# Set attention and a gated MLP on one core: three jobs of GpSimd given to VectorE, one sum in a bank of its own, the maxima of batches 1 to 3 without TensorE

## The chip, the core and the metric

The kernel runs on one core of a Trainium2 chip. A time is the device time of one execution in microseconds (us), the median of several. PE is TensorE, DVE VectorE, ACT ScalarE, POOL GpSimd, and SP the engine whose queue issues all DMAs here.

## The reference, cut to what matters

```python
B, N, m, C = 4, 12480, 32, 128          # x: (B, N, C); inducing: (m, C), float32

def mab(q, kv):
    s = (q @ kv.T) / sqrt(C)
    a = exp(s - s.max(-1));  a /= a.sum(-1) + 1e-9
    return a @ kv

h   = mab(inducing, x)                   # first attention: 32 queries over 12480 rows, for each batch
t   = mab(x, h)                          # second attention: 12480 queries over 32 rows
u   = t @ w_in                           # (49920, 128) @ (128, 2048)
out = (u * sigmoid(1.702 * u)) @ w_out   # (49920, 2048) @ (2048, 128)
```

`w_in` and `w_out` are float64, and the kernel takes each as a pair of 32-bit words and makes float32 of it on the chip ("decoding"). The product with `w_in` is folded into the second attention: `h @ w_in` is 32 rows a batch, so a token block's `u` is its 32 weights times that.

## The kernel before

**Tiling.** A batch's 12480 tokens are six "sups" of 2048 tokens and one of 192. The main work is 96 blocks of 512 tokens and 2 joint blocks of leftovers, each in 8 steps of two 128-column chunks of the 2048. In a step PE makes `ph` from the stacked weights `st` and `hw` (L484), ACT takes the gelu `g` (L508), ACT (L524) or DVE (L531) rounds it to `hi`, DVE takes the rest `lo` (L540), and PE adds three products per chunk into `pso` (L598 to L600). The first 12 steps use one full float32 product instead (L584).

**Order.** Nothing is scheduled on the chip. A planner in the kernel (`Plan`) holds jobs, each with an engine, an estimated time (`occ`, `lat`), a rank, a `wait` and a `gate`, and writes each engine's instructions out in the order in which its own clock would start them. `URGE` is how much earlier a job counts than it is ready, `BESIDE` lengthens a DVE job while POOL is at work, `counts["F"]` is the number of steps whose L484 is out. DVE, ACT and SP work in that order, one instruction after another.

**Opening** (batch 0). Transposed rows of `x` come by DMA; PE makes scores (`scores_of`, L302), DVE their maxima (L1213), PE and DVE spread the maximum of each of four `GROUPS` of sups (`group`, L1280 to L1292), ACT takes exponentials (L1304), DVE transposes them (L1317), and PE weighs the rows (`weigh`, L321) into `heap`, one PSUM bank in which each group has 128 columns. The rows in natural order (`xf`) are turned by PE and copied by ACT (`turn_of_x`, L1237, L1244), but for sup 5, which comes by a DMA (L1036). `combine` then adds the four sums with a factor each (L1353, L1355) and divides them (L1366). Beside this runs `weights(k)` for 8 pieces of 512 columns: seven operations of DVE, two of ACT and two of POOL (L1155, L1156; L1158 for the last).

**Batches 1 to 3** (`attention(b)`), spread among the steps: scores and maxima, then the maximum over sups and four partition groups, by DVE (L721), a PE product with the identity (L727), four operations of DVE on one row (L733, L737), a PE product back (L743) and one scaling (L749); then exponentials (L761), transposes (L781) and the weighing (L321), for which `loads_x` requests rows `xn` by DMA (L639), two sups at a time, in a ring of two buffers.

**Second attention** (`second`, `lay_out`): PE scores (L310); DVE transpose and maximum (L888, L895); POOL subtracts (L901); ACT exponentials (L926); DVE sums and inverts (L955 to L957); POOL scales, rounds and takes the rest (L967 to L969); DVE transposes both halves (L974, L977) into a ring `two` of two buffers; SP stacks them by 16 DMAs (L995). This is done for 27 parts, 23 of them of 512 columns and 4 small.

Of the kernel before, what the change touches and what calls it, by code (L numbers as in the profile page):

```python
# [10 lines left out]
F32R = mybir.dt.float32r  # L11
AF = mybir.ActivationFunctionType
# [4 lines left out]
P = 128  # L17
# [17 lines left out]
ROWS = 5,  # L35


def LOADS(xs, ws, n):
    return [xs[1], xs[2], ws[0], xs[3], ws[1], xs[4], xs[6], xs[5], *n, *ws[2:]]
# [4 lines left out]
URGE = 200.0  # L44
# [5 lines left out]
class Unit:  # L50


    def __init__(self, uses=1, ap=None, ready=None, parts=1):
        self.ap, self.uses, self.ready = ap, uses, ready
        self.parts = 0 if ready is not None else parts
        self.done, self.gone = 0.0, None
        self.by, self.soon = None, 0.0

# [50 lines left out]
class Plan:  # L109
# [4 lines left out]
    BESIDE = 0.34  # L114
# [39 lines left out]
    def step(self):  # L154
# [35 lines left out]
        if job.eng == "DVE":  # L190
            more = self.BESIDE * max(0.0, min(job.occ, self.free["POOL"] - s))
# [10 lines left out]
        for u in (*job.writes, *job.joins, *(u for _, u in job.takes)):  # L202
            u.made(job.eng, s + job.occ + more, end)
# [26 lines left out]


def on_pool(n):
    return 150 + 2.6 * n, 250 + 2.6 * n
# [3 lines left out]
def set_attention_then_moe(ctx: ExitStack, tc, xT, x, indT, w_in, w_out, outT):  # L237
# [77 lines left out]
    def weigh(pa, s, aT, xn, i, n):  # L315

        t0, g, w = sups[s]
        q = 32 * g
        for kk in range(w // 32):
            j = i % G  # L320
            pe_.matmul(  # L321
                pa[32 * j:32 * j + 32, 0:P], aT[0:q, kk, :], xn[0:q, kk],
                start=(i < G), stop=(i >= n - G),
            )
            i += 1
        return i
# [70 lines left out]
    x_units[0, 1].uses = 3  # L397
# [21 lines left out]
    r_2 = Ring(2, of_pool(p2, [P, TOK], "two", "two"))  # L419
# [212 lines left out]
    def loads_x(b, units, i0):  # L632
        for s in range(NS):
            t0, g, w = sups[s]
            u = units[s]
            for j in range(g):
                def emit(u=u, t0=t0, w=w, j=j):
# [7 lines left out]
                    rank=(1, b), gate=lambda: "n" in pools and counts["F"] >= i0, size=w * 512,  # L645
# [12 lines left out]
    def attention(b):  # L658
# [16 lines left out]
        yield Job("DVE", set_clear, 100, 200, rank=filler(), wait=tarry, gate=since(i0))  # L675
        s1 = [Unit(1) for _ in range(NS)]
# [40 lines left out]
        mx1 = psm.tile([P, 1], F32, tag="mx1", name="mx1")  # L717
        m1u, rowu, pa1, pa2 = Unit(), Unit(), Unit(), Unit()

        def most():  # L720
            dve.tensor_reduce(mx1, mx, axis=AX.X, op=ALU.max)  # L721

        yield Job("DVE", most, 100, 300, done, [], rank=filler(), wait=tarry)
        m1u.at(plan.free["DVE"] + 200)

        def turn():
            pe_.matmul(pa1.ap[0:1, 0:P], mx1, ident, start=True, stop=True)  # L727

        yield Job("PE", turn, 500, 700, [m1u], [], [(r_pa, pa1)], rank=(0, 0), slack=late(600, 1500))
        row = psm.tile([1, G, M], F32, tag="row", name="row", bufs=1)  # L730

        def rows():
# [6 lines left out]
        yield Job("DVE", rows, 600, 750, [pa1], rank=filler(), wait=tarry)  # L739
        rowu.at(plan.free["DVE"] + 150)  # L740

        def back():
            pe_.matmul(pa2.ap[:, 0:1], row.rearrange("p g m -> p (g m)"), one, start=True, stop=True)  # L743

        yield Job("PE", back, 450, 650, [rowu], [], [(r_pa, pa2)], rank=(0, 0), slack=late(600, 1500))
        nmx = psm.tile([P, 1], F32, tag="nmx", name="nmx")

        def least():
            dve.tensor_scalar(nmx, pa2.ap[:, 0:1], -scale, None, op0=ALU.mult)  # L749

        yield Job("DVE", least, 100, 250, [pa2], rank=filler(), wait=tarry)
# [19 lines left out]
        xn = [Unit(parts=sups[s][1]) for s in range(NS)]  # L771
        aT = [Unit() for _ in range(NS)]
        plan.spawn(loads_x(b, xn, i0 + 40))
# [98 lines left out]
    def second(b, *parts):  # L872
# [3 lines left out]
        for some in parts:  # L876
# [3 lines left out]
            def out(s, pa, u, due=due):  # L880
# [22 lines left out]
                occ, lat = on_pool(w)  # L903
                yield Job("POOL", less, occ, lat, [m2], [e], rank=(1, 0))
# [35 lines left out]
    def lay_out():  # L940

        for key in turns[1:]:
# [20 lines left out]
            ah, ahT, alT = Unit(1), Unit(2 * g), Unit(2 * g)  # L963

            def divide():
# [5 lines left out]
            yield Job("POOL", divide, 600 + 8.5 * w, 700 + 8.5 * w, [sm], [e], [(r_tr, ah)], rank=(0, 0))  # L971

            def turn_h():
                dve.transpose(ahT.ap[0:q, 0:w], ah.ap[0:q, 0:w].bitcast(F32))  # L974

            def turn_l():
                dve.transpose(alT.ap[0:q, 0:w], e.ap[0:q, 0:w])  # L977

            yield Job("DVE", turn_h, *on_dve(w), [ah], [], [(r_2, ahT)], **by_then(due), slack=late(300, 1200))
            yield Job("DVE", turn_l, *on_dve(w), [e], [], [(r_2, alT)], **by_then(due))  # L980
            for j in range(g):
# [9 lines left out]
                for r in range(G):  # L991
                    src = alT if r % 2 else ahT

                    def emit(st=st, r=r, j=j, at=at, w=w, src=src):
                        nc.sync.dma_start(  # L995
                            st.ap[32 * r:32 * r + 32, at:at + w].bitcast(F32),
                            src.ap[32 * j:32 * j + 32, 0:w],
# [12 lines left out]
    def opening_loads():  # L1010
# [19 lines left out]
        for what, k in order:  # L1030
            if what == "n":
# [13 lines left out]
                else:  # L1045
                    plan.spawn(iter([job]))
            elif what == "x":
# [19 lines left out]
    def divided(c, cols):  # L1067
        due = 16 + 2 * c - 4
# [7 lines left out]
        def top():  # L1076
            act.copy(wh.rearrange("p c d -> p (c d)")[:, cols], wf[:, cols])

        def rest():
            dve.tensor_sub(wlf[:, cols], wf[:, cols], whf[:, cols].bitcast(F32))  # L1080

        u = Unit()
        yield Job("ACT", top, *on_act(512), [wf_units[c]], [], joins=[w_out_units[c], u], rank=rank, wait=tarry, gate=since(due))
        yield Job("DVE", rest, *on_dve(512), [u], [], joins=[w_out_units[c]], rank=rank, wait=tarry)

    def weights(k):
# [8 lines left out]
        whole = inner or c < WHOLE  # L1095
        into, done = (w_in_sb, w_in_units[c]) if inner else (wf, wf_units[c]) if whole else (whf, w_out_units[c])
# [10 lines left out]

        def square():
# [4 lines left out]
        def low_1():  # L1113
            dve.tensor_scalar(t.ap, hi(), 0x1FF, 12, op0=ALU.bitwise_and, op1=ALU.logical_shift_left)

        yield Job("DVE", low_1, 360, 470, [raw], takes=[(rings["t"], t)], rank=rank, wait=tarry)

        def low_2():
            dve.scalar_tensor_tensor(lo(), lo(), 20, t.ap, op0=ALU.logical_shift_right, op1=ALU.bitwise_or)

        yield Job("DVE", low_2, 610, 730, [], [t, raw], rank=rank, wait=tarry)

        def floats():
            act.activation(lo_f(), lo(), AF.Copy, scale=2.0 ** -32)

        low = Unit()
        plan.spawn(iter([Job("ACT", floats, 530, 700, [], [raw], joins=[low], rank=rank, wait=tarry)]))

        def top_1():
            dve.tensor_scalar(t.ap, hi(), 3, 0x3FFFF000, op0=ALU.logical_shift_left, op1=ALU.bitwise_and)  # L1130

        yield Job("DVE", top_1, 360, 450, [raw], [t], rank=rank, wait=tarry)
# [7 lines left out]
        def guard():  # L1140
            dve.scalar_tensor_tensor(
                into[:, cols], sq.ap, LEAST, t.ap.bitcast(F32), op0=ALU.is_ge, op1=ALU.mult
            )

        yield Job("DVE", guard, 610, 730, [sq, t], [], joins=[top] + [done] * (not whole), rank=rank, wait=tarry)
        sq.used(0.0)

        def powers():
            dve.tensor_scalar(hi(), into[:, cols].bitcast(I32), -(1 << 23), None, op0=ALU.bitwise_and)
# [3 lines left out]
        def lower():  # L1153
            if whole:
                nc.gpsimd.tensor_mul(hi_f(), lo_f(), hi_f())  # L1155
                nc.gpsimd.tensor_add(into[:, cols], into[:, cols], hi_f())  # L1156
            else:
                nc.gpsimd.tensor_mul(wlf[:, cols], lo_f(), hi_f())  # L1158

        cost = 3500 if whole else 1750  # L1160
        yield Job("POOL", lower, cost, cost + 150, [low, raw, raw], joins=[done], rank=rank)
        if whole and not inner:
            plan.spawn(divided(c, cols))
        decoded[0] += 1
        decoded[1] += at < SPLIT
# [32 lines left out]
    def scores_of(s):  # L1198
# [10 lines left out]
        occ = 4.1 * w * 0.42  # L1209
# [5 lines left out]
        yield Job("DVE", most, *on_dve(w), [pa], [], joins=[mx_units[s]], rank=(0, 1 + s))  # L1215
# [8 lines left out]
    def turn_of_x(s):  # L1224
# [4 lines left out]
        for k0 in range(0, w // 32, 8):  # L1229
# [10 lines left out]
            yield Job("PE", emit, 112 * n_, 112 * n_ + 250, there, [], [(r_ph, ph)], rank=(2, s), wait=350.0)  # L1240
# [23 lines left out]
    heap = Unit(99)  # L1264
# [3 lines left out]
    def group(g):  # L1268
# [4 lines left out]
        urge = -URGE if last else 0.0  # L1273
# [50 lines left out]
    def weighs():  # L1324
        for g in groups:
# [3 lines left out]
            for s in order:  # L1329
                def emit(s=s, i=i, nb=nb, g=g):  # L1330
                    a = aT_units[s].ap.rearrange("p (k m) -> p k m", m=M)
                    i[0] = weigh(heap.ap[:, g * P:(g + 1) * P], s, a, xf_units[s].ap, i[0], nb)

                occ = 67.0 * (sups[s][2] // 32)
# [320 lines left out]
```

## Time and profile before

| | us |
|---|---|
| median of 3 runs (1601.36 to 1602.05) | 1601.56 |
| the profiled execution | 1601.29 |
| its span, first to last instruction | 1599.2 |
| PE busy | 1575.1 |
| DVE busy | 1358.1 |
| ACT busy | 1319.7 |
| POOL busy | 176.5 |

The 2.1 us between the profiled execution's time and its span lie before the first and behind the last instruction. A busy PE is not PE at its peak: a matmul's record is longer than the distance to the next.

### The profile page before, as it was taken

To read this page: it belongs to the slowest core of one execution; us is meant where nothing else is said; L and a number is where in the kernel's file an instruction comes from. 1 tells how busy PE (TensorE), PEld (TensorE's weight loads), DVE (VectorE), ACT (ScalarE), POOL (GpSimd) and SP (SyncE) were. 2 spreads that over 40 slices of the span, in tenths; PEclk is the share of its full clock that TensorE was granted. 3 is DMA by queue.
4 is the path that set the end of the run, shared out by engine and by line. 5 is a ranking of instruction groups with operands and counts; after the bars stand their busy time and mean duration, and the time that the engine had idled before them with its cause. 6 is when DMAs were issued, how large, how long until landed. Compare 5 with 4: busy or idle time off the path is not lost. (4 is left out here: it accounts for less than half of the span.)

```text
span 1599.2 us, 21638 instructions
## 1 busy us (share of the span) xinstructions
PE 1575.1 (98%) x7715; PEld 1224.2 (77%) x7715; DVE 1358.1 (85%) x1537; ACT 1319.7 (83%) x1490; POOL 176.5 (11%) x129
## 2 busy tenths in 40 slices
PE   8899999999999999999999999999999999999998
PEld 6467777778887787787777777788778888888887
DVE  6989888888887888879889888788888888888886
ACT  5688888888888888788888888788988888888886
POOL 1321011020210100102011001011110110110100
PEclk9999999999999999999999999999999999999999
DMA  6262174431124226442013274410101101111100
GB/s 253 92 226 72 48 129 87 144 106 40 45 75 144 60 60 117 97 126 86 27 47 134 87 138 77 124 34 27 40 25 47 38 30 37 40 34 33 40 27 20
DMA packets 83435, 124.55 MB, mean 78 GB/s; under 512 B 12096, under 2 KB 50560, under 8 KB 77952
## 3 DMA queue, kind: packets, MB, share of 16 engines
q1 hardware_dynamic: 83328, 123.17, 27.9%
q8 instruction: 62, 1.02, 0.3%
q14 instruction: 45, 0.37, 0.1%
HBM read 69.91 MB, written 25.56 MB: 60 GB/s over the span
## 5 line engine op out<-in xcount | busy, mean ns | idle before, releaser
L540 DVE TENSOR_TENSOR lo<-g,hi 128x1024 fp32r<-128x1024 f32 (+1 forms) x772 | 965.0, 1262 | 167.2 <-ACT hi L524 153.4
L508 ACT ACTIVATE g<-ph 128x1024 f32<-128x1024 f32 (+1 forms) x784 | 801.9, 1029 | 231.3 <-PE ph L484 122.1
L598 PE MATMUL pso<-hi,wl 128*128 128x512 f32 (+1 forms) x1544 | 608.3, 394 | 0.0
L600 PE MATMUL pso<-hi,wh 128*128 128x512 f32 (+1 forms) x1544 | 606.5, 393 | 0.0
L599 PE MATMUL pso<-lo,wh 128*128 128x512 f32 (+1 forms) x1544 | 604.4, 391 | 0.8 <-DVE lo L540 0.8
L484 PE MATMUL ph<-st,hw 128*128 128x512 f32 x1536 | 473.0, 400 | 6.8 <-DVE hw L1438 2.2
L524 ACT ACTIVATE hi<-ph 128x1024 fp32r<-128x1024 f32 x458 | 469.5, 1029 | 2.8 <-PE pso L600 2.4
L484 PEld LDWEIGHTS ph<-st,hw 128*128 128x128 f32 x1536 | 280.5, 188 | 104.8 <-ACT hi L524 15.3
L598 PEld LDWEIGHTS pso<-hi,wl 128*128 128x128 f32 x1544 | 290.1, 188 | 70.1 <-issue 2.9
L600 PEld LDWEIGHTS pso<-hi,wh 128*128 128x128 f32 x1544 | 290.6, 188 | 66.1
L599 PEld LDWEIGHTS pso<-lo,wh 128*128 128x128 f32 x1544 | 290.4, 188 | 65.7 <-DVE lo L540 1.1
L531 DVE CAST hi<-g 128x1024 fp32r<-128x1024 f32 (+1 forms) x314 | 222.7, 709 | 27.7 <-ACT g L508 17.3
L967 POOL TENSOR_TENSOR e<-e,sm 128x512 f32<-128x512 f32 x23 | 36.5, 1588 | 1068.4 <-DVE sm L957 1068.4
L560 ACT COPY ob<-pso 128x512 f32<-128x512 f32 x73 | 43.4, 595 | 13.9 <-PE pso L600 13.8
L969 POOL TENSOR_TENSOR e<-e,t 128x512 f32<-128x512 f32 x23 | 45.3, 1969 | 1.8
L901 POOL TENSOR_TENSOR e<-e,m 128x512 f32<-128x512 f32 x23 | 32.3, 1406 | 58.0 <-DVE m L895 57.0
L968 POOL CAST t<-e 128x512 fp32r<-128x512 f32 x23 | 32.3, 1404 | 1.5
L563 DVE COPY ob<-pso 128x512 f32<-128x512 f32 (+1 forms) x25 | 17.1, 683 | 10.4 <-PE pso L600 9.9
L302 PE MATMUL pa<-xt,indT_sb 128*32 128x512 f32 x192 | 23.7, 599 | 0.7 <-DMA xt<-in_xT 0.7
L321 PE MATMUL pa<-xn,t 128*32 128x128 f32 (+1 forms) x594 | 19.5, 275 | 4.2 <-DMA xn<-in_x 4.2
L310 PE MATMUL pa<-xt,hT 128*32 128x512 f32 x184 | 22.9, 599 | 0.0
L584 PE MATMUL pso<-g,wf 128*128 128x512 f32 x48 | 22.7, 594 | 0.0
(170 smaller groups left out, 482.9 us busy)
## 6 DMA issues: line engine op xcount, KB each, us to landing
xt<-in_xT SPq DMA_DIRECT2D x42, 1024.0 KB, 6.5
out_T<-ob SPq DMA_DIRECT2D x96, 256.0 KB, 2.0
st<-two SPq DMA_DIRECT2D x368, 64.0 KB, 2.0
xn<-in_x SPq DMA_DIRECT2D x72, 256.0 KB, 6.4
hw<-t SPq DMA_DIRECT2D x48, 64.0 KB, 2.7
raw<-in_w_in SPq DMA_DIRECT2D x4, 512.0 KB, 9.1
raw<-in_w_out SPq DMA_DIRECT2D x4, 512.0 KB, 5.3
xt<-in_xT SPq DMA_DIRECT2D x2, 512.0 KB, 3.9
```

What stands on the lines that cost most here:

```text
L484: pe_.matmul(ph[:, c, at:at + w], u.ap[:, ch % 4 * P:(ch % 4 + 1) * P], st[:, at:at + w], start=True, stop=True,)
L508: act.activation(gs[i].ap[:, :, 0:w], phs[i].ap[:, :, 0:w], AF.Gelu_apprx_sigmoid)
L524: act.activation(his[i].ap[:, :, 0:w], phs[i].ap[:, :, 0:w], AF.Gelu_apprx_sigmoid)
L531: dve.tensor_copy(his[i].ap[:, :, 0:w], gs[i].ap[:, :, 0:w])
L540: dve.tensor_sub(los[i].ap[:, :, 0:w], gs[i].ap[:, :, 0:w], his[i].ap[:, :, 0:w].bitcast(F32))
L560: act.copy(ob.ap[:, 0:w], pso.ap[:, 0:w])
L598: pe_.matmul(o, wl[:, ch, :], hi, start=(ch == 0), stop=False)
L599: pe_.matmul(o, wh[:, ch, :], lo, start=False, stop=False)
L600: pe_.matmul(o, wh[:, ch, :], hi, start=False, stop=(ch == NCH - 1))
L901: nc.gpsimd.tensor_sub(e3, e3, m2.ap[0:q, 0:k].unsqueeze(2).broadcast_to([q, k, M]))
L967: nc.gpsimd.tensor_mul(e3, e3, sm.ap[0:q, 0:nb].unsqueeze(2).broadcast_to([q, nb, M]))
L969: nc.gpsimd.tensor_sub(e.ap[0:q, 0:w], e.ap[0:q, 0:w], ah.ap[0:q, 0:w].bitcast(F32))
```

## The change

1. `weights`: POOL's two operations go to DVE, and the two DVE operations that joined the low bits (L1114, L1119) go: ACT now reads 16 of the low word's bits (`lo_16`). The last piece is decoded into a temporary and split afterwards as the others are (`divided`).
2. `second` and `lay_out`: subtraction and scaling go to DVE; the scaled weights are transposed once, ACT (or DVE) rounds the result, DVE takes the rest in place. POOL has no work left.
3. Opening: the last group's sum goes to a buffer of its own (`tail`, of the ring that `ph` uses); half of sup 4's rows comes by a DMA of 1024 rows of 512 bytes (`HALF`) in place of 8 PE transposes and an ACT copy; the last group's maxima count as urgent.
4. `attention`: four DVE reductions of 32 partitions each, one over their results and four scalings in place of L721 to L749; `loads_x` may be placed from step `i0 + 40` on, ahead of the maxima in the thread, and the planner reckons its DMAs 2.4 times as long.
5. The planner: `URGE` 200 to 500, `BESIDE` gone, 110 ns (`AFTER`) between a DVE result and a DVE job that uses it, some PE times.

```diff
-URGE = 200.0
+URGE = 500.0
-    BESIDE = 0.34
+    AFTER = 110.0
...
+    return [xs[1], xs[2], ws[0], xs[3], ws[1], xs[4], xs[6], xs[5], *n, ("h", HALF), *ws[2:]]
...
-                    rank=(1, b), gate=lambda: "n" in pools and counts["F"] >= i0, size=w * 512,
+                    rank=(1, b), gate=lambda: "n" in pools and counts["F"] >= i0, size=2.4 * w * 512,
...
+        xn = [Unit(parts=sups[s][1]) for s in range(NS)]
+        plan.spawn(loads_x(b, xn, i0 + 40))
...
         def most():
-            dve.tensor_reduce(mx1, mx, axis=AX.X, op=ALU.max)
...
-            pe_.matmul(pa1.ap[0:1, 0:P], mx1, ident, start=True, stop=True)
...
-            dve.tensor_reduce(
-                row[:, 0, :], pa1.ap[0:1, 0:P].rearrange("p (g m) -> p m g", g=G), axis=AX.X, op=ALU.max
-            )
-            for j in range(1, G):
-                dve.tensor_copy(row[:, j, :], row[:, 0, :])
...
-            pe_.matmul(pa2.ap[:, 0:1], row.rearrange("p g m -> p (g m)"), one, start=True, stop=True)
...
-            dve.tensor_scalar(nmx, pa2.ap[:, 0:1], -scale, None, op0=ALU.mult)
+            for j in range(G):
+                dve.tensor_reduce(tops[:, j:j + 1], mx[M * j:M * j + M], axis=AX.X, op=ALU.max)
+            dve.tensor_reduce(tops[:, G:G + 1], tops[:, 0:G], axis=AX.X, op=ALU.max)
+            for j in range(G):
+                dve.tensor_scalar(nmx[M * j:M * j + M], tops[:, G:G + 1], -scale, None, op0=ALU.mult)
...
-                    nc.gpsimd.tensor_sub(e3, e3, m2.ap[0:q, 0:k].unsqueeze(2).broadcast_to([q, k, M]))
+                    dve.tensor_sub(e3, e3, m2.ap[0:q, 0:k].unsqueeze(2).broadcast_to([q, k, M]))
...
-                nc.gpsimd.tensor_mul(e3, e3, sm.ap[0:q, 0:nb].unsqueeze(2).broadcast_to([q, nb, M]))
-                nc.gpsimd.tensor_copy(ah.ap[0:q, 0:w], e.ap[0:q, 0:w])
-                nc.gpsimd.tensor_sub(e.ap[0:q, 0:w], e.ap[0:q, 0:w], ah.ap[0:q, 0:w].bitcast(F32))
...
-                dve.transpose(ahT.ap[0:q, 0:w], ah.ap[0:q, 0:w].bitcast(F32))
...
-                dve.transpose(alT.ap[0:q, 0:w], e.ap[0:q, 0:w])
...
+                dve.tensor_mul(e3, e3, sm.ap[0:q, 0:nb].unsqueeze(2).broadcast_to([q, nb, M]))
...
+                dve.transpose(aT.ap[0:q, 0:w], e.ap[0:q, 0:w])
...
+                act.copy(ah.ap[0:q, 0:w], aT.ap[0:q, 0:w])
...
+                dve.tensor_sub(aT.ap[0:q, 0:w], aT.ap[0:q, 0:w], ah.ap[0:q, 0:w].bitcast(F32))
...
+                rows = x[t0 + g * w // 2:t0 + g * w, :]
+                nc.sync.dma_start(u.second, rows.rearrange("(k p) c -> p k c", p=P))
...
-            dve.tensor_scalar(t.ap, hi(), 0x1FF, 12, op0=ALU.bitwise_and, op1=ALU.logical_shift_left)
...
-            dve.scalar_tensor_tensor(lo(), lo(), 20, t.ap, op0=ALU.logical_shift_right, op1=ALU.bitwise_or)
...
-            act.activation(lo_f(), lo(), AF.Copy, scale=2.0 ** -32)
+            act.activation(lo_f(), lo_16(), AF.Copy, scale=2.0 ** -36)
...
-                nc.gpsimd.tensor_mul(hi_f(), lo_f(), hi_f())
-                nc.gpsimd.tensor_add(into[:, cols], into[:, cols], hi_f())
+            dve.tensor_mul(lo_f(), lo_f(), hi_f())
...
+            dve.tensor_add(into(), into(), lo_f())
...
+    def sum_of(g):
+        if g == groups[-1]:
+            return tail.ap.rearrange("p c t -> p (c t)")[:, 0:P]
+        return heap.ap[:, g * P:(g + 1) * P]
```

## Rows read from the trace of the kernel before

**Rows 1.** The page: span, and each engine's busy time and instructions.
```profile
span 1599.2 us, 21638 instructions
PE 1575.1 (98%) x7715; PEld 1224.2 (77%) x7715; DVE 1358.1 (85%) x1537; ACT 1319.7 (83%) x1490; POOL 176.5 (11%) x129
```

**Rows 2.** Busy time of each engine in four stretches, granted clock, DMA share, GB/s.
```profile
0.00:37.00 37.00, 32.13 (x386) 24.39 (x387) 22.88 (x71) 21.97 (x39) 5.41 (x10) 1.00 0.74 274
37.00:80.00 43.00, 36.19 (x137) 18.66 (x136) 40.40 (x74) 28.27 (x40) 15.25 (x12) 1.00 0.24 86
80.00:100.00 20.00, 18.54 (x92) 9.71 (x92) 16.82 (x24) 18.00 (x22) 9.89 (x9) 1.00 0.72 258
100.00:1590.00 1490.00, 1483.22 (x7084) 1167.72 (x7083) 1277.96 (x1372) 1250.84 (x1390) 145.96 (x99) 1.00 0.27 71
```

**Rows 3.** PE's waits from 100 us on: total, times, longest.
```profile
PE pa L321 <- DMA xn<-in_x: 4.2, 2, 2.3
...
PE pso L599 <- DVE lo L540: 0.8, 1, 0.8
```

**Rows 4.** Timeline of PE, 210 to 232 us: start, duration, idle before.
```profile
212.78 0.39 PE L599 MATMUL pso<-lo,wh 128*128 128x512 f32 x1
213.00 0.40 PE L600 MATMUL pso<-hi,wh 128*128 128x512 f32 x1
213.33 0.38 PE L727 MATMUL pa<-ident,mx 128*1 128x128 f32 x2
213.64 1.20 PE L484 MATMUL ph<-st,hw 128*128 128x512 f32 x4
...
217.53 0.38 PE L743 MATMUL pa<-one,row 1*128 1x1 f32 x2
...
230.42 1.08 PE L321 MATMUL pa<-xn,t 128*32 128x128 f32 x32 [2.32 <-DMA xn<-in_x]
```

**Rows 5.** Timeline of SP's queue, 195 to 245 us.
```profile
216.90 6.54 SPq L639 DMA_DIRECT2D xn<-in_x  x8
```

**Rows 6.** Busy time and granted clock behind that wait.
```profile
231.50:235.50 4.00, 4.00 (x12) 3.14 (x12) 3.36 (x5) 1.94 (x2) 0.00 (x0) 0.57 1.24 189
```

**Rows 7.** Timeline of DVE, 0 to 60 us.
```profile
17.21 0.43 DVE L1130 TENSOR_SCALAR t<-raw 128x512 int32<-128x512 int32 x1
...
24.43 0.23 DVE L1281 TENSOR_SCALAR tops<-mask,mx 128x4 f32<-128x4 f32 x1
...
27.61 0.64 DVE L1213 TENSOR_REDUCE mx<-pa 128x1 f32<-128x512 f32 x1
...
28.48 0.77 DVE L1281 TENSOR_SCALAR tops<-mask,mx 128x4 f32<-128x4 f32 x1
...
33.41 0.35 DVE L1353 TENSOR_SCALAR hu<-pso,factor 128x128 f32<-128x128 f32 x1 [0.67 <-PE pso L321]
...
35.04 0.35 DVE L1355 SCALAR_TENSOR_TENSOR hu<-pso,factor,hu 128x128 f32<-128x128 f32 x1
```

**Rows 8.** Timeline of PE, 0 to 65 us.
```profile
25.79 1.06 PE L302 MATMUL pa<-xt,indT_sb 128*32 128x512 f32 x8
...
35.53 0.46 PE L1366 MATMUL pa<-rsb,hu 128*128 128x128 f32 x2 [0.88 <-DVE hu L1355]
```

**Rows 9.** Groups by line and shape, whole run: busy us, mean ns, idle before.
```profile
L540 DVE TENSOR_TENSOR lo<-g,hi 128x1024 fp32r<-128x1024 f32 x756 | 949.6, 1269 | 162.8 <-ACT hi L524 149.4 <-PE pso L600 1.1 <-issue 0.2
...
L974 DVE STREAM_TRANSPOSE two<-t 128x512 f32<-128x512 f32 x23 | 16.1, 700 | 0.0
...
L1130 DVE TENSOR_SCALAR t<-raw 128x512 int32<-128x512 int32 x8 | 7.0, 880 | 0.2
L1119 DVE SCALAR_TENSOR_TENSOR raw<-raw,t 128x512 int32<-128x512 int32 x8 | 7.0, 878 | 0.3
...
L851 DVE TENSOR_TENSOR t<-pa,t 128x512 f32<-128x512 f32 x3 | 2.0, 683 | 0.0
```

**Rows 10.** Timeline of DVE, 1300 to 1320 us, where POOL rests.
```profile
1300.02 1.23 DVE L540 TENSOR_TENSOR lo<-g,hi 128x1024 fp32r<-128x1024 f32 x1 [0.59 <-ACT hi L524]
```

More of the change, by code (lines that the diff above doesn't have):

```diff
@@ L202, in step @@
         for u in (*job.writes, *job.joins, *(u for _, u in job.takes)):
-            u.made(job.eng, s + job.occ + more, end)
+            u.made(job.eng, s + job.occ + more + self.AFTER * (job.eng == "DVE"), end)
         for u in job.reads:
@@ L1065, in opening_loads, with divided @@
         loaded.append(True)
-    def divided(c, cols):
-        due = 16 + 2 * c - 4
+    def divided(c, cols, whole, ready, over):
+        due = 16 + 2 * c - 4 if c < WHOLE else 4 * c - 2
         def rank():
@@ L1076, in top @@
         def top():
-            act.copy(wh.rearrange("p c d -> p (c d)")[:, cols], wf[:, cols])
+            act.copy(whf[:, cols], whole())
         def rest():
-            dve.tensor_sub(wlf[:, cols], wf[:, cols], whf[:, cols].bitcast(F32))
+            dve.tensor_sub(wlf[:, cols], whole(), whf[:, cols].bitcast(F32))
+            over()
         u = Unit()
-        yield Job("ACT", top, *on_act(512), [wf_units[c]], [], joins=[w_out_units[c], u], rank=rank, wait=tarry, gate=since(due))
+        yield Job("ACT", top, *on_act(512), [ready], [], joins=[w_out_units[c], u], rank=rank, wait=tarry, gate=since(due))
         yield Job("DVE", rest, *on_dve(512), [u], [], joins=[w_out_units[c]], rank=rank, wait=tarry)
@@ L1141, in guard, with add, finish @@
             dve.scalar_tensor_tensor(
[L1142 removed]
+                into(), sq.ap, LEAST, t.ap.bitcast(F32), op0=ALU.is_ge, op1=ALU.mult
             )
[L1145 removed]
+        yield Job(
+            "DVE", guard, 610, 730, [sq] if kept is None else [sq, t], [t] if kept is None else [], joins=[top],
+            rank=rank, wait=tarry,
+        )
         sq.used(0.0)
         def powers():
[L1149 removed]
+            dve.tensor_scalar(hi(), into().bitcast(I32), -(1 << 23), None, op0=ALU.bitwise_and)
         yield Job("DVE", powers, 360, 470, [top], [raw], joins=[], rank=rank, wait=tarry)
         def lower():
[L1154 to L1163 removed]
+            dve.tensor_mul(lo_f(), lo_f(), hi_f())
+        yield Job("DVE", lower, 610, 730, [low], [raw], rank=rank, wait=tarry)
+        def add():
+            dve.tensor_add(into(), into(), lo_f())
+        yield Job("DVE", add, 610, 730, [raw, raw], [], joins=[done], rank=rank, wait=tarry)
+        if not inner:
+            plan.spawn(divided(c, cols, into, done, finish if kept is None else lambda: None))
+        decoded[1] += at < SPLIT
+        if inner or kept is not None:
+            finish()
+    def finish():
         decoded[0] += 1
[L1165 removed]
         if decoded[0] == 2 * G:
@@ L1213, in most @@
             dve.tensor_reduce(mx[0:q, s:s + 1], pa.ap[0:q, 0:w], axis=AX.X, op=ALU.max)
-        yield Job("DVE", most, *on_dve(w), [pa], [], joins=[mx_units[s]], rank=(0, 1 + s))
+        yield Job("DVE", most, *on_dve(w), [pa], [], joins=[mx_units[s]], rank=(0, 1 + s), wait=-URGE * (s in GROUPS[-1]))
         if s == NS - 2:
@@ L1228, in turn_of_x @@
         x_ = x_units[0, s]
-        for k0 in range(0, w // 32, 8):
+        for k0 in range(0, BLK // 2 if s == HALF else w // 32, 8):
             n_ = min(8, w // 32 - k0)
@@ L1322, in group, with weighs @@
             plan.spawn(exponential(s))
-    def weighs():
-        for g in groups:
+    def weighs(some):
+        for g in some:
             nb = blocks(GROUPS[g])
@@ L1331, in emit @@
                     a = aT_units[s].ap.rearrange("p (k m) -> p k m", m=M)
-                    i[0] = weigh(heap.ap[:, g * P:(g + 1) * P], s, a, xf_units[s].ap, i[0], nb)
-                occ = 67.0 * (sups[s][2] // 32)
-                first_ = g == 0 and s == order[0]
+                    i[0] = weigh(sum_of(g), s, a, xf_units[s].ap, i[0], nb, xf_units[s].second)
+                occ = 60.0 * (sups[s][2] // 32)
+                new = s == order[0] and ([(r_po, heap)] if g == 0 else [(r_ph, tail)] if g == groups[-1] else [])
                 yield Job(
                     "PE", emit, occ, occ + 250, [aT_units[s], xf_units[s]], [],
-                    [(r_po, heap)] if first_ else [], joins=[h_units0[g]], rank=(1, s),
-                    wait=0.0 if g == len(GROUPS) - 1 else 200.0,
+                    new or [], joins=[h_units0[g]], rank=(1, s), wait=0.0 if g >= len(GROUPS) - 2 else 200.0,
                 )
@@ L1369, in add_up @@
             heap.used(plan.now, 99)
+            tail.used(plan.now, 99)
             hu_ = hT_units[0]
@@ L1563, in emit @@
             act.activation(warm, one, AF.Gelu_apprx_sigmoid)
-        yield Job("ACT", emit, 60, 200, gate=lambda: fasts[0] == 2, rank=(0, 9), table="gelu")
+        yield Job("ACT", emit, 60, 200, gate=lambda: fasts[0] == 2 and fasts[1], rank=(0, 9), table="gelu")
     def attentions():
```

106 lines of the change are left out of this document (51 added, 55 removed).

## The prediction

> **What bounds the kernel now.** I read the page's table of engines first: PE is busy in 1575.1 of the span's 1599.2 us, so no change on another engine can give more than PE's idle time, what PE loses at a lower clock, and PE work that is struck out [rows 1]. The busy times by stretch say where the idle time lies [rows 2]: 37.00 - 32.13 = 4.9 us up to 37 us, 6.8 from 37 to 80, 1.5 from 80 to 100, 6.8 in the 1490 us after that; the rest, 1599.2 - 1590 - 5.0 = 4.2, lies behind the last matmul, in the final copy and store, which the change leaves alone. So the kernel has two regimes. Up to 100 us it hangs on chains: DVE is busy 40.40 of the 43 us from 37 to 80 [rows 2], and PE waits for what DVE hands over. After 100 us PE is the bound, DVE and ACT have 212 and 239 us to spare, and of the 6.8 us a single cause takes 4.2: two waits of the weighing for rows of x [rows 3]. I then read the timelines around that wait and around the end of the opening's chain, and last the groups by shape for durations.
>
> One page of the Trainium skill speaks against this change. Perfetto Trace Analysis, section Identifying the Most-Contended Engine, holds matmul busy time for a poor measure and goes by weight loads; by that, PE stands at 77% and DVE, at 85%, is the engine to spare, not to load [rows 1]. This trace does not bear it out for the stretch after 100 us, where PE is idle 0.5% and DVE 14% [rows 2]; before 80 us it does. What it would make of the time is the third rival.
>
> **The maxima of batches 1 to 3.** L727 and L743 go, three times each. Between L600 and the L484 behind L727 lie 13.64 - 13.00 = 0.64 us, between two products 0.22 [rows 4]: 0.42 us for each of the six, 2.5 us. PE is the bound there, so this comes off whole; at the least it is nothing, should the gap have been filled by slack, and it cannot be more than the gap. I take 2.4. DVE does nine small operations instead of six, none longer than the 0.23 us of L1281 alone [rows 7], so 0.7 us per batch at most, hidden in its 14% of idle time.
>
> **The rows requested ahead.** The thread of batch 1 could place its requests only behind the maxima: SP issues eight from 216.90 to 223.44 [rows 5], beside L743, and at 230.42 PE has waited 2.32 us for the last of them [rows 4]. A second wait of the kind makes it 4.2 us; there are two in three batches [rows 3]. In the new order the first two sups may be requested from step 40 of the batch before on, whether or not the maxima are through, and the planner expects the others later, so that it places PE's use of them later too. I take the 4.2 us as gone; if the wait only moves to the next two sups, which still need a free buffer, none of it goes. The clock adds to this. Behind the wait of 2.32 us the granted clock of a stretch of 4 us is 0.57 [rows 6], so PE lost 4 x 0.43 = 1.7 us more at its lower level, 1.2 in place of 2.4 GHz. That goes too: 5.9 us, bounds 0 and 5.9. On SP's queue the eight requests (6.54 us of issuing) stand in front of stacks and stores; the stacks are placed 24 steps ahead of use, and a step is eight matmuls at a distance of 0.22 us [rows 4], so 42 us cover them. Without that cover it would be up to 6.5 us in each batch.
>
> **The opening.** Three pieces. The last sup's scores are done at 25.79 + 1.06 = 26.85, but their maximum begins at 27.61 [rows 7, 8], behind other DVE work; as an urgent job it can begin 0.7 earlier. L1281 took 0.77 us with POOL at work and 0.23 without [rows 7]: 0.5. Then the end: L1353 begins at 33.41, released by the last weighing, though it reads another group's sum, since all four lie in one bank; three more additions follow, the last at 35.04, and PE goes on at 35.53 [rows 7, 8]. With a bank of its own for the last group the first three of these four operations fit beside the weighing: of the 35.04 - 33.41 = 1.63 us they take 3 x 0.35, and the other 0.6 is the inversion (L1405 to L1407), which DVE has to do in any case: 1.0. Sum 2.2. The half of sup 4 that comes by DMA spares ACT a copy and PE eight transposes; I give it nothing, since its half megabyte stands in the queue behind the other rows and must be there in time. Bounds 0 and 4.
>
> **Decoding.** Per piece DVE loses L1114 (like L1130 alone, 0.43 us) and L1119 (0.88 as it ran), and gains two operations with two operands on 512 columns, at 0.68 [rows 7, 9]: about even. What it wins is the slowing: L1130 takes 0.88 us on the mean and 0.43 alone [rows 7, 9], so 0.45 per piece on that line. Six of eight pieces are decoded between 37 and 80 us: 2.7 us from a DVE that is the pace there. That is a third of the 8.3 us that PE is idle from 37 to 100, which is the upper bound. Against it stand about one more operation for the last piece and, from 76 us on, five subtractions at 0.68 and the first part's scaling and rest, less a transpose, 4.1 us; DVE has 3.2 us idle from 80 to 100 [rows 2] and wins back what POOL's 9.9 us there cost it. I take 2.7, bounds -2 (a loss) and 7.
>
> **The second softmax, 100 us on.** A large part adds subtraction, scaling and rest (3 x 0.68) and one transpose for two (-0.70): 1.35 us of DVE, some 31 us for 23 parts and less for the four small ones, and a copy on ACT, which has the 239 us named above. In return L540 falls from a mean of 1.269 to the 1.23 it takes with POOL at rest [rows 9, 10]: 756 x 0.039 = 29 us. DVE stays where it is, 86%. No PE time either way, covered by DVE's idle time and by the six buffers of `hi` and `lo` ahead of PE; without that cover see the third rival.
>
> **The sum.** 2.4 + 5.9 + 2.2 + 2.7 = 13.2 us off the profiled execution's 1601.29 (which lies 0.3 below the median of 1601.56, too little to correct for): 1588.1, said as 1588, which is 0.8% faster. PE being the bound after 100 us, what the opening saves goes through to the end.
>
> **The rivals.**
> - *The opening gives nothing*: other DVE work fills what POOL's absence frees, or the extra half megabyte holds the last rows back. For it speaks that DVE is at 94% there and gets new work; against it that POOL's operations lie on the chain itself. Then only 2.4 + 5.9 come off: 1593.
> - *The wait for the rows moves*, to the next two sups of the same batch, whose buffer is only free when the first are weighed. For it: the ring has two buffers still, and one batch of three has no such wait, so a few us decide. Against it: PE's visits are now placed later. Then 13.2 - 5.9: 1594, and 1601, no change, together with the rival above and a wait as long again.
> - *Slower: DVE becomes late in bursts.* Each part's rest on DVE stands behind ACT's copy, which can stand behind a gelu; what is queued behind it on DVE is `lo`, and PE waits for that. The trace has this wait once in the stretch, 0.8 us [rows 3]. From the point where the six buffers are used up, 27 parts cost 27 x 0.8 = 21.6 us, and the time is 1588 + 21.6 = 1610. Against it speak the 212 us of idle DVE time and the relief. This is also what the skill's page on trace analysis would have one expect.
>
> **How the numbers follow.** Forecast 0.63; opening without gain 0.14; wait moved 0.10, of which a third ends at no change; slower 0.09; the rest, 0.04, no change for a mix of small gains and losses. A measurement of this kernel tells about 0.2%, 3.2 us, from no change. Faster 0.63 + 0.14 + 0.07 = 0.84, less 0.03 for a forecast that falls far short: 0.81. Same 0.03 + 0.04 and two of those three hundredths, 0.09; slower 0.09 and the third, 0.10. The likeliest case alone reaches from 1582 (opening 4, decoding 7) to 1595 (decoding a loss of 2, opening nothing). For 8 in 10 the range takes in both faster rivals, and at the lower end 2 us for what half of sup 4 may give: 1580 to 1597.
>
> **What would show it.** No POOL rows but the first memsets; no PE wait of L321 for `xn` and a granted clock of 1.0 from 200 to 240 us; no L727 and L743; L1353 no longer released by the last weighing; the division L1366, at 35.53 us before, near 33.3; each L1130 at 0.43; PE idle from 37 to 100 us near 5.5 where it was 8.3; L540 at a mean of 1.23. Wrong would make it: PE waits for `lo` at the parts, a new wait of L321, an L484 that waits for `st`, a new stretch at the lower clock.

## The result, and the profile after

The kernel after takes 1588.15 us (1586.52 to 1588.47, four executions) against 1601.68 (1601.36 to 1602.05): ratio 0.9913, 95% interval 0.9896 to 0.9931. The forecast was 1588.0. The runs show that this agreement is partly luck: one term has the wrong sign, two are too small, and the errors cancel.

The page's engine table and the busy times by stretch of the kernel after answer to [rows 1, 2]; columns as there.

```profile
span 1584.7 us, 21430 instructions
...
PE 1570.1 (99%) x7693; PEld 1225.1 (77%) x7693; DVE 1337.1 (84%) x1616; ACT 1324.6 (84%) x1502; POOL 0.7 (0%) x6
...
0.00:37.00 37.00, 32.00 (x385) 23.93 (x386) 22.02 (x72) 21.58 (x40) 0.70 (x6) 1.00 0.81 288
37.00:80.00 43.00, 39.84 (x159) 20.31 (x161) 40.36 (x83) 33.66 (x45) 0.00 (x0) 1.00 0.36 132
80.00:100.00 20.00, 19.20 (x103) 11.71 (x96) 18.79 (x30) 19.38 (x24) 0.00 (x0) 1.00 0.72 249
100.00:1575.00 1475.00, 1473.04 (x7030) 1164.65 (x7029) 1254.71 (x1433) 1249.05 (x1395) 0.00 (x0) 1.00 0.27 70
```

PE idles 4.0 us from 37 to 100 (8.3 before) and 2.0 behind 100 (6.8 before). DVE took over POOL's work and is still busy 21 us less. A busy window does not say how fast PE goes, though. So I also compared the two traces by work done: the time at which the same number of main products (those with `hw`, `wl` and `wh`) had started. By that the kernel after leads by 0.8 us at the first L482 (L484 before), by 7.1 near 115 us, by 10 near 300, and by 14.0 at the end.

PE's waits from 100 us on ([rows 3] before) hold no row for `xn`, and the granted clock is 1.0 in each stretch above. The end of the opening, on DVE and PE, answers to [rows 7, 8] (L1207 is the maximum, L1352 and L1354 the sums, L1365 the division, L1551 the copy of the first `st`):

```profile
26.91 0.69 DVE L1207 TENSOR_REDUCE mx<-pa 128x1 f32<-128x512 f32 x1 [0.34 <-PE pa L299]
27.83 0.23 DVE L1281 TENSOR_SCALAR tops<-mask,mx 128x4 f32<-128x4 f32 x1
31.85 0.34 DVE L1352 TENSOR_SCALAR hu<-pso,factor 128x128 f32<-128x128 f32 x1
33.53 0.35 DVE L1354 SCALAR_TENSOR_TENSOR hu<-ph,factor,hu 128x128 f32<-128x128 f32 x1
40.09 0.69 DVE L1551 CAST st<-ph 128x512 fp32r<-128x512 f32 x1
...
33.93 0.49 PE L1365 MATMUL pa<-rsb,hu 128*128 128x128 f32 x2
38.95 0.63 PE L1542 MATMUL ph<-ident,e 128*128 128x128 f32 x4 [1.24 <-DVE e L1526]
40.93 1.17 PE L482 MATMUL ph<-st,hw 128*128 128x512 f32 x4 [1.34 <-DVE st L1551]
```

The division is 1.6 us earlier, but the first product with `hw` only 0.8 (41.76 before): `st` is now copied by DVE, behind another operation. Part of either figure can be chance: the runs of the rows alone and of the maxima alone have the same instructions as the kernel before up to that product, and in their profiled executions it starts 1.0 and 0.3 us earlier than in that of the kernel before. `lo`, by shape ([rows 9] before), has a mean of 1221 ns where it had 1269:

```profile
L538 DVE TENSOR_TENSOR lo<-g,hi 128x1024 fp32r<-128x1024 f32 x756 | 914.7, 1221 | 189.7 <-ACT hi L522 176.2 <-PE pso L598 2.3 <-PE pso L597 0.9
```

### The profile page after: what moved, and what is told of

Its sections match the earlier page's. It is cut to its first block, busy times and chain, and to the rows that moved or that the text cites. A ratio compares the mean times of both kernels' runs of the same rounds, so it can differ in the third digit from the quotient of the medians.

```text
span 1584.7 us, 21430 instructions
## 1 busy us (share of the span) xinstructions
PE 1570.1 (99%) x7693; PEld 1225.1 (77%) x7693; DVE 1337.1 (84%) x1616; ACT 1324.6 (84%) x1502; POOL 0.7 (0%) x6
## 3 DMA queue, kind: packets, MB, share of 16 engines
q8 instruction: 62, 1.02, 0.3%
## 5 line engine op out<-in xcount | busy, mean ns | idle before, releaser
L538 DVE TENSOR_TENSOR lo<-g,hi 128x1024 fp32r<-128x1024 f32 (+1 forms) x772 | 929.9, 1216 | 194.5 <-ACT hi L522 180.7
L522 ACT ACTIVATE hi<-ph 128x1024 fp32r<-128x1024 f32 (+1 forms) x460 | 474.2, 1033 | 4.7 <-PE pso L598 4.3
L482 PE MATMUL ph<-st,hw 128*128 128x512 f32 x1536 | 465.7, 399 | 4.1 <-ACT hi L522 1.6
L482 PEld LDWEIGHTS ph<-st,hw 128*128 128x128 f32 x1536 | 282.6, 188 | 97.4 <-ACT hi L522 10.2
L529 DVE CAST hi<-g 128x1024 fp32r<-128x1024 f32 (+1 forms) x312 | 210.7, 682 | 13.7 <-ACT g L506 9.6
L558 ACT COPY ob<-pso 128x512 f32<-128x512 f32 (+1 forms) x70 | 41.6, 595 | 10.0 <-PE pso L598 9.6
L561 DVE COPY ob<-pso 128x512 f32<-128x512 f32 x28 | 19.2, 685 | 8.1 <-PE pso L598 8.0
L318 PEld LDWEIGHTS pa<-xn,t 128*32 128x32 f32 (+1 forms) x594 | 15.6, 110 | 4.4 <-issue 3.6
L961 DVE TENSOR_TENSOR t<-t,two 128x512 f32<-128x512 f32 (+1 forms) x27 | 16.7, 619 | 1.3 <-ACT two L950 1.1
L862 DVE STREAM_TRANSPOSE e<-pa 128x512 f32<-128x512 f32 x23 | 15.9, 703 | 0.5 <-PE pa L307 0.4
L945 DVE STREAM_TRANSPOSE t<-e 128x512 f32<-128x512 f32 x23 | 16.2, 706 | 0.1
```

Of the source, the lines that this page charges most:

```text
L318: pe_.matmul(pa[32 * j:32 * j + 32, 0:P], aT[0:q, kk, :], xn[0:q, kk] if second is None or kk < BLK // 2 else second[0:q, kk - BLK // 2], ...
L482: pe_.matmul(ph[:, c, at:at + w], u.ap[:, ch % 4 * P:(ch % 4 + 1) * P], st[:, at:at + w], start=True, stop=True,)
L522: act.activation(his[i].ap[:, :, 0:w], phs[i].ap[:, :, 0:w], AF.Gelu_apprx_sigmoid)
L529: dve.tensor_copy(his[i].ap[:, :, 0:w], gs[i].ap[:, :, 0:w])
L538: dve.tensor_sub(los[i].ap[:, :, 0:w], gs[i].ap[:, :, 0:w], his[i].ap[:, :, 0:w].bitcast(F32))
L558: act.copy(ob.ap[:, 0:w], pso.ap[:, 0:w])
```

## The experiments

The kernel before, run beside each of the three groups below, took 1600.92, 1601.53 and 1601.44 us. "Distance" is from the start of one main product to that of the next.

### One part of the change alone, on the kernel before

**Rows.** Edit: `loads_x` ahead of the maxima and its reckoned size, nothing else.

```diff
-                    rank=(1, b), gate=lambda: "n" in pools and counts["F"] >= i0, size=w * 512,
+                    rank=(1, b), gate=lambda: "n" in pools and counts["F"] >= i0, size=2.4 * w * 512,
...
+        xn = [Unit(parts=sups[s][1]) for s in range(NS)]
+        plan.spawn(loads_x(b, xn, i0 + 40))
...
```

> The kernel before with the requests for rows ahead of the maxima and the 2.4 in the planner alone. Theory (the prediction's step): both waits of L321 for xn go and with them the stretch at the lower clock, 5.9 us: 1595.7. Rival (the wait moves to the next two sups): a wait of L321 for xn of 1 to 4 us stays, the time is 1599 to 1602.

1594.69 us, ratio 0.9957 (0.9943 to 0.9972): 6.2 faster. No wait for `xn` is left, and from 200 to 240 us, the granted clock (last but two) is 1.00:

```profile
200.00:240.00 40.00, 39.68 (x223) 30.25 (x222) 34.19 (x43) 33.49 (x45) 3.11 (x2) 1.00 0.43 85
```

**Maxima.** Edit: the nine DVE operations in place of L721 to L749.

```diff
...
-            pe_.matmul(pa1.ap[0:1, 0:P], mx1, ident, start=True, stop=True)
...
-            pe_.matmul(pa2.ap[:, 0:1], row.rearrange("p g m -> p (g m)"), one, start=True, stop=True)
...
+                dve.tensor_reduce(tops[:, j:j + 1], mx[M * j:M * j + M], axis=AX.X, op=ALU.max)
...
```

> The kernel before with the maxima of batches 1 to 3 on DVE alone. Theory: six slots of 0.42 us go, 2.4 us, and the requests, still behind the maxima, come some us earlier: 1599.2 with the waits for xn, down to 1594 if that is enough to end them. Rival: the gap was slack, 1601.5.

1604.06 us, ratio 1.002 (1.001 to 1.003): 3.1 slower, where both forecasts had a gain or no change. One visible cause is that PE comes to the weighing 7.5 us earlier (219.48 against 227.02), and the requests for its rows, still behind the maxima, only 6.7 (210.25 against 216.90 in [rows 5]) and more slowly. SP's queue, PE's timeline, and the window around the end of PE's wait, with a clock of 0.52:

```profile
210.25 7.56 SPq L639 DMA_DIRECT2D xn<-in_x  x8
...
225.02 1.93 PE L321 MATMUL pa<-xn,t 128*32 128x128 f32 x32 [4.47 <-DVE lo L540]
...
222.00:229.00 7.00, 3.98 (x37) 3.19 (x38) 3.51 (x4) 1.57 (x2) 0.00 (x0) 0.52 1.21 200
```

The `lo` named there is only the last event: the eight requests are issued up to 217.81 us, the last of them lands at 224.78, and `xn` is what is late. The other cause showed in the last set.

**Opening.** Edit: part 3 of the change, with the constant of 500 that its urgent jobs use.

```diff
...
+    plan.spawn(weighs(groups[:-1]))
+    plan.spawn(weighs(groups[-1:]))
```

> The kernel before with the opening's part alone (own bank for the last sum, half of sup 4 by DMA, urgency), POOL still decoding. Theory: the division begins 1.0 to 1.7 us earlier and the whole kernel ends 1 to 2 us earlier: 1599.5 to 1600.5. Rival: DVE's decoding is the pace behind it and swallows the gain: 1601.5, with PE idle 1 to 2 us longer between 37 and 100 us.

1597.61 us, ratio 0.9974 (0.9964 to 0.9985): 3.3 faster and more than the forecast, though PE runs 6.8 us at the lower clock from 56.5 us on.

**Decoding.** Edit: part 1.

```diff
...
-                nc.gpsimd.tensor_mul(hi_f(), lo_f(), hi_f())
...
+            dve.tensor_mul(lo_f(), lo_f(), hi_f())
...
```

> The kernel before with the weights decoded without GpSimd alone. Theory A (DVE paces the stretch from 37 to 80 us and POOL slowed it and stood in its chain): the first L598 comes 5 us earlier and the time is 1596 to 1598. Theory B (only what all of GpSimd's absence gives counts, the prediction's 2.7 us at most): 1599. Rival: DVE is as full as before, 1601.5.

1605.3 us, ratio 1.0028 (1.0018 to 1.0037): 4.4 slower, which none of the three forecasts had. DVE has less to do from 37 to 80 us (34.84 busy) and PE waits all the same, ahead of the folding of pieces of `w_in` (L1420), and loses clock (0.88):

```profile
55.08 1.13 PE L1420 MATMUL pa<-w_in_sb,hT 128*128 128x512 f32 x2 [1.96 <-DVE e L1482]
63.65 2.08 PE L1420 MATMUL pa<-w_in_sb,hT 128*128 128x512 f32 x2 [2.00 <-DVE w_in_sb L1157]
...
37.00:80.00 43.00, 35.15 (x123) 18.01 (x123) 34.84 (x73) 27.16 (x38) 2.10 (x2) 0.88 0.25 86
```

So it is the order and not DVE's load: in the kernel after, L1418, the same folding, stands at 47.65, 54.99 and 65.10 us without a wait, beside a DVE that is busy for 40.36 us. Nor does the clock decide it: executions of this run with a mean granted clock of 0.998 took as long (1605.3 to 1605.4) as the profiled one with 0.996 (1605.3).

### One part undone in the kernel after

**Decoding** (the operations of part 1 back on POOL):

> The kernel after with the decoding of before: GpSimd's two operations, the two VectorE operations that joined the low bits and the last piece without a temporary are back; planner, opening, maxima, rows and second softmax stay as in after. Theory of the prediction (terms add): the term of 2.7 us goes back, 1588.1 + 2.7 = 1590.8, PE idle from 37 to 100 us about 6.7 where after has 4.0, the operation at 0.42 us back near 0.88. Rival (the parts work only together): the 37 to 100 us stretch loses all it won from decoding, planner and part one of the second softmax, about 6 us, 1594, since GpSimd's slow operations stand in a chain that the new planner no longer reckons with. Second rival: it loses nothing, 1588, since decoding without GpSimd alone on the kernel before cost 4.4 us and the gain came from elsewhere.

1595.04 us, ratio 0.9959 (0.9944 to 0.9974): 6.9 slower than after, near the 1594 of the first rival. The first product with `hw` comes at 45.59 instead of 40.93 us, and DVE's small operations take about as long as those of POOL that run beside them. DVE, then POOL:

```profile
35.52 1.02 DVE L1141 TENSOR_SCALAR raw<-w_in_sb 128x512 int32<-128x512 int32 x1
38.96 1.24 DVE L1512 TENSOR_TENSOR e<-e,sm 128x128 f32<-128x128 f32 x1
...
35.22 1.04 POOL L1147 TENSOR_TENSOR raw<-raw 128x512 f32<-128x512 f32 x1 [33.91 <-DVE raw L1141]
38.77 1.28 POOL L1148 TENSOR_TENSOR w_in_sb<-w_in_sb,raw 128x512 f32<-128x512 f32 x1
```

The scaling L1512 takes 0.29 us in the kernel after (L1514), the line L1141 0.41 (L1139).

**Second softmax** (part 2 back on POOL):

> The kernel after with the second softmax of before: GpSimd subtracts, scales, rounds and takes the rest, VectorE transposes both halves into the ring of two buffers. Theory of the prediction: no PE time either way behind 100 us; VectorE sheds some 31 us of work and pays some 29 us by slower operations; the operation that makes lo is back at a mean near 1.27 us; 1588 within 1.5. Rival one: the first part of batch 0 lies on the chain before 100 us, where GpSimd was busy 9.9 of 20 us, and its return costs 2 to 4 us: 1590 to 1592, all of it before 110 us. Rival two (VectorE late in bursts in after): the return of GpSimd wins time after 100 us, 1585 or less.

1591.94 us, ratio 0.9939 (0.9923 to 0.9956): 3.8 slower than after, where the forecast had no difference. The intervals of the two ratios just touch (0.9923 and 0.9931); the single executions lie 3.2 us apart at least. `lo` is back at 1268 ns. Of the profiled difference, 2.3 us stand at 100 us and 5.3 at the end, so 3 us come behind 100 us, where the first rival had next to nothing. In the profiled execution PE runs 3.4 us from 41 us on at the lower clock, which makes 1.6 of the 5.3; the profiled execution of the kernel after has no such stretch (clock 1.0), its other three have a mean clock of 0.999:

```profile
41.50:44.50 3.00, 3.00 (x13) 2.71 (x12) 1.45 (x5) 2.39 (x3) 0.00 (x0) 0.50 0.00 0
```

**Opening** (part 3 back, the constant of 500 stays):

> The kernel after with the opening of before: one bank for the four sums, all of sup 4 by TensorE and ScalarE, the last group's maxima not urgent, the planner's tie and waits there as before; the setting of 500 and the 110 ns stay. Theory of the prediction: 2.2 us come back, 1590.3, all of it before 45 us. Rival one: only what the first ph product moved comes back (41.76 against 40.93, 0.8 us): 1589. Rival two: the order from 37 to 80 us gets as uneven as in the run of decoding alone (two waits of near 2 us for pieces of w_in, then a lower clock): 1592 or more.

1589.36 us, ratio 0.9924 (0.9909 to 0.9938): 1.2 slower than after, between the theory and the first rival. The two intervals (0.9909 to 0.9938 and 0.9896 to 0.9931) overlap over most of their length, so this difference is not clear of noise.

**The planner's constant** (`URGE` 500 to 200):

> The kernel after with one constant of the planner changed back, 500 to 200: how much earlier an urgent job counts than it is ready. Nothing that the engines execute differs but its order. Theory of the prediction, which gave the setting no term: 1588 within 1. Rival: the setting is what makes the decoding's order even, and without it PE waits twice for pieces of w_in from 45 to 65 us as in the run of decoding alone: 1592 to 1595.

1590.22 us, ratio 0.9928 (0.9913 to 0.9942): 2.1 slower, which neither forecast had, and with intervals that overlap, too. By work done 2.8 us of the profiled difference stand at 45 us and 3.6 at the end; PE runs 6.8 us from 39.5 us on at the lower clock, and no wait for `w_in` came back.

### What makes the parts work, and two surprises

**Decoding with the planner's constants**, on the kernel before:

```diff
-URGE = 200.0
+URGE = 500.0
...
-    BESIDE = 0.34
+    AFTER = 110.0
...
-        tie = (-URGE if rank == 1 else -URGE / 2) if early else 200.0
+        tie = (-URGE if rank == 1 else -URGE / 2) if early else 0.0
```

> The kernel before with the new decoding and the planner's new constants (500 for 200, 110 ns between dependent VectorE jobs, no lengthening beside GpSimd, the tie of the later blocks of the first joint softmax); opening, maxima, rows and second softmax as before. Decoding alone cost 4.4 us there. Theory (the planner's constants make the decoding's order even): the two waits for pieces of w_in from 55 to 64 us go, and decoding wins its 2.7 us: 1598.9 at most. Rival (the new decoding needs a VectorE without GpSimd beside it and an opening that leaves room): still 1601 or more, with the waits for w_in.

1598.3 us, ratio 0.9984 (0.9974 to 0.9993): the loss of 4.4 becomes a gain of 3.1, and the long waits ahead of the folding of `w_in` are gone, as the theory has it.

**The same with the second softmax on DVE**:

> As the run before it, with the second softmax on VectorE too, so that GpSimd has no work; opening, maxima and rows as before. Theory (additive, from the runs that undo one part): the second softmax is worth 3.8 us and decoding with the planner 2.7 to 6.9, so 1592 to 1595. Rival: decoding and softmax without the new opening give nothing, 1600 or more, and the gain ahead of 100 us is the opening's room.

1588.65 us, ratio 0.9922 (0.9907 to 0.9937). That is 9.7 us from the second softmax, more than the forecast, and 12.8 of the change's 13.5 us, without its maxima, its rows and its opening.

**Maxima undone in the kernel after**:

> The kernel after with the maxima of batches 1 to 3 of before, two products of TensorE a batch, while rows of x are still requested ahead of them. Theory of the prediction: six gaps of 0.42 us come back, 2.5 us: 1590.6, and no wait for rows. Rival: the gaps had been covered, and the maxima by themselves give nothing or cost, as in the run of the maxima alone (3.1 us slower, with late rows): 1588 or less.

1581.74 us, ratio 0.9878 (0.9864 to 0.9893): 6.4 us *faster* than after, the best of all. PE's timeline shows the two products back at the price forecast, (208.95 - 208.31) - 0.23 = 0.4 us each (L727; L743 alike):

```profile
208.31 0.40 PE L598 MATMUL pso<-hi,wh 128*128 128x512 f32 x1
208.64 0.38 PE L727 MATMUL pa<-ident,mx 128*1 128x128 f32 x2
208.95 0.73 PE L482 MATMUL ph<-st,hw 128*128 128x512 f32 x2
```

What outweighs them is the pace of the main products. The same window, 1260 to 1560 us, where PE makes main products alone (the other engines still work on four parts of the second softmax), for before, after and this kernel, in this order:

```profile
1260.00:1560.00 300.00, 300.00 (x1296) 242.58 (x1296) 256.76 (x256) 250.13 (x272) 20.86 (x12) 1.00 0.13 36
```

```profile
1260.00:1560.00 300.00, 300.00 (x1292) 242.40 (x1291) 252.74 (x264) 249.78 (x273) 0.00 (x0) 1.00 0.12 34
```

```profile
1260.00:1560.00 300.00, 300.00 (x1301) 243.85 (x1300) 254.60 (x264) 249.23 (x271) 0.00 (x0) 1.00 0.12 34
```

PE is 100% busy in all three and does 1296, 1292 and 1301 products. Over all traces, worked out from the products' starts (columns: products in that window; from 110 to 1560 us the mean distance of those nearer than 300 ns, and by how much the others together exceed 231 ns each; time):

```
second softmax  maxima   run                      products  mean ns  excess us  time us
POOL            old      before                     1296    231.57    13.8      1601.6
POOL            old      rows alone                 1296    231.63    12.9      1594.7
POOL            old      opening alone              1295    231.62    12.3      1597.6
POOL            old      decoding alone             1295    231.60    12.9      1605.3
POOL            old      decoding, planner          1296    231.55    12.8      1598.3
DVE             old      the same, softmax          1299    231.48     7.0      1588.7
DVE             old      after, maxima undone       1301    231.43     8.1      1581.7
POOL            new      maxima alone               1291    232.55    11.3      1604.1
POOL            new      after, softmax undone      1291    232.57    11.5      1591.9
DVE             new      after, decoding undone     1292    232.58     5.8      1595.0
DVE             new      after, opening undone      1292    232.61     6.5      1589.4
DVE             new      after, constant undone     1291    232.59     7.0      1590.2
DVE             new      after                      1292    232.61     6.7      1588.2
DVE             new      after, small products      1292    232.62     6.6      1586.2
```

Two things can be read off. With the new maxima each product stands 1.0 to 1.2 ns further off, comparing runs with the second softmax on the same engine: for some 6,100 products behind 110 us an estimated 6 to 7 us. With the second softmax on POOL the long distances cost 11 to 14 us, on DVE 6 to 8.

**Eight small products** of the identity ahead of the first block of the kernel after:

```diff
+            if j == 0:
+                spins(4, ph.ap[:, 0, 0:P])
...
+                if i == 0:
+                    spins(4, ph[:, 0, 0:P])
```

> The kernel after with eight more small products of TensorE, of the identity with itself: four ahead of the first block's transposes, where TensorE waits 1.24 us, and four ahead of the first product with hw, where it waits 1.34 us; their results are overwritten by the product that follows. The planner is not told of them, so that nothing else moves. Theory: the execution with a profile, 1586.5, had a granted clock of 1.0 throughout, and the kernel's other executions, near 1588.2 at a mean clock of 0.999, lose some 1.7 us in one stretch at the lower level as the one at 41.4 to 44.8 us in the run with the second softmax undone; with PE busy in those two waits the stretch does not come: median 1586.5, clock 1.0. Rival: the stretch has nothing to do with these waits, or the small products delay the first product: 1588.2 or more.

1586.16 us (1585.96 to 1586.42), ratio 0.9905 (0.9889 to 0.9922), 2.0 below the median of after and at a clock of 1.0 in all four executions, as the theory has it; the intervals overlap, so it is the clock that tells the two apart. PE is busy 41.66 of the 43 us where it was 39.84:

```profile
37.00:80.00 43.00, 41.66 (x178) 22.11 (x178) 40.36 (x83) 33.64 (x45) 0.00 (x0) 1.00 0.37 133
```

## Why the prediction was right, and where it was not

**The frame** held in part. PE sets the pace behind 100 us, but "no change on another engine can give more than PE's idle time" was wrong: a product's record lasts 0.40 us and the next starts after 0.23, so a product can start 0.17 us late with PE still shown busy. Such delays, 3.6 us that no idle time shows, were the largest part that I can place of what the second softmax gave back, and the slower pace that came with the new maxima shows in no busy time.

**The rows requested ahead**, 5.9: right in size and in cause, 6.2 alone, wait and clock both gone. The requests on SP's queue delayed nothing that the trace shows. The rival of the moved wait did not come; late rows came back, with a wait of 4.5 us, only in the run with the new maxima alone.

**The maxima**, 2.4: the term itself was priced rightly, 0.4 us for each of six products, and yet the part costs 6.4 net in the kernel after and 3.1 on the kernel before. The step that failed is "this comes off whole". In all seven kernels with the new maxima, the main products are slower, by an estimated 6 to 7 us in all. By work done, the kernel with the maxima undone gains 5.0 us on the kernel after from 115 us to the end, which is about that pace less 2.4 for the six gaps; the rest of the 6.4 I can't place. What the part changes for them is the place of the buffers: the `row` buffer of 512 bytes a partition goes and smaller ones come, and in the program's table of buffers `g`, `hi` and `lo` begin 448 bytes lower (the first `g` at byte 144864 instead of 145312), in exactly these seven. From 1260 to 1560 us the distance behind a product with `wl` is 240 ns or more for 82 of 322 in the kernel after and for none of 325 with the maxima undone; over all traces it is 24 to 40% in the seven and none in the others. That the part slows the products is shown; that the place of the buffers does it is argued from this pairing. A kernel that moves the buffers and nothing else was not run, and it stays open which of the buffers matters, and why.

**The opening**, 2.2: 3.3 alone, 1.2 when undone; in the kernel after the division is 1.6 earlier, the first product 0.8. Right to within its bounds, but the 1.2 are not clear of noise, and up to 1 us of the 1.6 can be chance. Between the division and the first product, time was lost to the copy of `st` behind another operation of DVE.

**Decoding**, 2.7: mis-sized. Alone it is a loss of 4.4, with the planner's constants a gain of 3.1, and undone in the kernel after it costs 6.9. I priced DVE's time per piece, but its worth hangs on the order: on when the first pieces of `w_in` are folded. The planner's constants, which I gave no term, turn 4.4 lost into 3.1 won. The forecast for the slowing was right, L1111 takes 0.42.

**The second softmax**, 0: the largest error of size, 3.8 when undone and 9.7 when added to decoding. The DVE account was right (`lo` from 1269 to 1221 ns; I had 1230) and "covered by the six buffers of `hi` and `lo`" was not. The wait that mattered was for `ph`, which ACT reads. With decoding, the planner and POOL, 11 first products of a step came over 300 ns after the `wh` product ahead of them, 3.4 us in excess; with DVE 2, with 0.4. Most of the rest is between two products with `hw`, 8.2 against 5.4. In all, long distances went from 12.8 to 7.0 us, 2.2 of the difference as idle time of PE, and the waits of the weighing for its rows from 4.1 to 2.3; the rest of the 9.7 I can't place.

**The rivals.** DVE late in bursts did not come: PE waits for `lo` once, 0.5 us, ahead of 100 us. Its price was misread, too: the one wait of 0.8 us of [rows 3] ends at 99.52 us, so the kernel before has none behind 100 us. The Trainium skill's page Perfetto Trace Analysis, section Identifying the Most-Contended Engine, judges TensorE not by its matmuls' busy time but by its weight loads (here 77%) and its share of the peak, the other engines by their busy time (DVE 85%), and has the most contended one optimized first; that would have spared DVE. Here the work put on DVE made DVE's total smaller, 1358.1 to 1337.1 us. The opening without gain fell too: 7.1 us are won by 115 us, against 4.9 forecast.

**The sum.** Forecast 2.4 + 5.9 + 2.2 + 2.7 + 0. The parts do not add: decoding, planner and second softmax give 12.8 together; maxima, rows and opening on top of these 0.5 to 0.7, since the rows' 6 us (part of which the new order had already won) and the opening pay for the maxima. The best kernel run is the change without its maxima, 1581.74.

## What to carry to other kernels

Time an edit by undoing it in the final kernel as well as by adding it to the first one: here the two gave opposite signs for decoding, and a total that agreed hid a part worth dropping. Where PE reads 100% busy, count its products in a window of equal work before calling it as fast as it can be. And when an edit adds or removes a buffer, look at what that moves behind it.

## What the runs showed of the hardware

- **The pace of TensorE changed by 0.7%** (1301 products against 1292 in 300 us, granted clock 1.00 and PE fully busy in both) between two kernels whose main loop is written the same. The Trainium skill's page SBUF — State Buffer, section SBUF: two separate sides, says that among engines only the pair of ports that VectorE and GpSimd share is contended, and that PE never waits. GpSimd has no work in either run, so these runs do not bear that out, if the buffers' place is the cause.
- **TensorE's clock near 40 us.** The granted clock is 0.5 (1.2 in place of 2.4 GHz) for 3.4 us in the profiled executions with the second softmax, the opening or the maxima undone and with decoding and the planner, and for 6.8 us with the constant undone and with the second softmax added to decoding. These stretches begin between 39.5 and 44.0 us, during or just behind waits of PE of 1.2 to 2.5 us; one of 3.4 us cost 1.6 (second softmax undone, by work done). The same waits do not always end so: three of four executions of the kernel after have a mean granted clock of 0.999, the profiled one 1.0 and 1.6 us less. With PE kept busy in its two waits of 1.24 and 1.34 us all four took 1586.0 to 1586.4 at 1.0, while three of four with the maxima undone, measured beside them with the same waits, had 0.999.
- **GpSimd beside VectorE**: a DVE operation of 0.29 us in the kernel after took 1.24 beside one of POOL with decoding undone, one of 0.41 took 1.02.
